# Attention with a position bias and a split-float16 feed-forward layer on one core: six spread maxima, each as one product with the unit matrix instead of a transpose and a spreading product

## The chip, the cores and the metric

The kernel runs on one core of a Trainium2 chip. The metric is device microseconds of one execution. The core has a matrix engine (TensorE, PE in the profile, its weight loads PEld), VectorE (DVE), ScalarE (ACT), GpSimd (POOL) and SyncE (SP), which here only issues transfers. Each engine works through its own instructions in the order in which they stand, and the engines wait for each other by semaphores.

## The reference

```python
def _attn_ref(q, k, v, w1, b1, w2):                      # q, k, v: 4 x 8 x 576 x 64
    scores = scale * np.matmul(q, k.transpose(0, 1, 3, 2))
    ...
    x = (psi_rel / psi_i)[..., None]                     # from the distance of two positions
    bias = np.maximum(x @ w1 + b1, 0.0) @ w2             # one bias table for each of 8 heads
    scores = scores + bias.transpose(2, 0, 1)[None, :, :, :]
    attn = softmax(scores)
    return np.matmul(attn, v)

def _moe_ref(x, w_in, w_out):                            # x: 2304 x 512, d_ff: 2048
    h = x @ w_in
    g = h * np.clip(h + 3.0, 0.0, 6.0) / 6.0
    return g @ w_out
```

The weights `w_in` and `w_out` come as 64-bit floats, which the kernel takes apart itself.

## The kernel before, in words

**Work.** Attention runs in tiles of 128 queries by 576 keys of one head, 144 tiles in 32 units. Of one tile: the scores `s_ps` (line 532 for the first 32 tiles of batches 0 and 1, line 552 for the others), bias and row minimum on DVE (line 564, 0.75 us), the exponential on ACT (line 575), a transpose of the result (`t_ps`, line 623, put away by ACT in line 626; later tiles by a DMA, line 640), and the product with v (`pv_ps`, lines 665 and 711). The attention result of 256 or 320 queries of all four head pairs is the input `x` of one pass of the feed-forward layer: 16 tiles `h_ps` of 12 products (line 786), the clipped product in lines 776, 769, 763 and 765, then four tiles `o_ps` of 48 products (line 809). There are eight such passes.

**Preparation of the weights.** Float16 products need a value and a remainder, so each operand is scaled by a power of two and split into a high part (lines 118 to 124) and a low part (line 141). `w_in` is loaded in 8 chunks and `w_out` in 8 chunks of 1024 KB (line 247). A chunk is treated by ACT (line 257), POOL (258), and DVE (265, 268, 271), gives a row scale (209, 164, 214) and is split into `wi` or `wo`. The loads of `w_out` land in places that the work on earlier chunks has to free first: the first two chunks go into the part of `wo` in which the last two chunks of `w_in` were staged, so each of these two loads waits for the low split (line 141) of one of them; the fourth waits for DVE's line 271 of the first, and so on.

**The spread maximum.** Six times the kernel needs the largest value over all 128 partitions, in every partition: for `v` of the batches 0 to 3 (`v_scale`), for the row scales of `w_in` and for those of `w_out` (`row_ratio`). `spread_max` (lines 145 to 161) takes the maximum of each partition (`m`, line 147), turns the column into a row on TensorE (153), takes the maximum of the row on DVE (155, one value `g`), spreads it over the partitions with a product with a row of ones (157) and copies it out of PSUM (160) into `p`. All this goes through one bank of the pool `w`, which has two banks at that time and also holds `h_ps` and `pv_ps`. With `p` of `w_in` the rows of `x` are scaled (line 1110), with `p` of `w_out` the 16 tiles `g` of the first pass (line 122 on DVE, 124 on ACT), before its first `o_ps`.

**What sets the order.** The kernel is written as generators: `v_scale`, `w_in_prep`, `w_out_prep`, the bias tables and the feed-forward layer are each advanced by a step, up to their next `yield`, from the loop over attention tiles. A scheduler then puts the instructions of each engine into an order by these places and by the times that it assumes for them. From tile 39 on the order of PE stands as written, from tile 45 on that of SP. All loads are issued by SP, in order.

Of the kernel before, what the change touches and what calls it, by code (L numbers as in the profile page):

```python
# [10 lines left out]
F32 = mybir.dt.float32  # L11
# [4 lines left out]
ALU = mybir.AluOpType  # L16
AX = mybir.AxisListType
# [16 lines left out]
def attention_moe_kernel(  # L34
# [16 lines left out]
    nc = tc.nc  # L51
# [7 lines left out]
    const = ctx.enter_context(tc.tile_pool(name="const", bufs=1))  # L59
# [30 lines left out]
    def w_bank(name):  # L90

        if name == "o_ps":
            out_open[:] = [True, 0]
        elif out_open[0] and four[0]:
            while out_open[0] and out_open[1] == 3:
                next(queue[0])
            out_open[1] += 1
        return pools["ps_w"].tile([128, 512], F32, tag="w", name=name)

    open_psum(stack_p, 3, 2)  # L100
    eye_sb = const.tile([128, 128], F32, name="eye_sb")
# [2 lines left out]
    wo = big.tile([128, 2, KF, DM], F16, name="wo")  # L104
    bias_d = [dr_p.tile([H, min(128, S - i), S], F32, name=f"bias{i}") for i in range(0, S, 128)]

    ones_sb = const.tile([1, 128], F32, name="ones_sb")
    b1_sb = const.tile([128, 1], F32, name="b1_sb")
    w2_sb = const.tile([128, 32], F32, name="w2_sb")
    tq = [const.tile([128, 2, 128], F32R, name=f"tq{r}") for r in range(2)]  # L110
# [34 lines left out]
    def spread_max(parts, name, mask=False):  # L145
        m = const.tile([128, 1], F32, tag="m", bufs=2, name=f"m_{name}")
        nc.vector.tensor_reduce(out=m, in_=parts, op=ALU.max, axis=AX.X)
        if mask:
            mb = m.bitcast(U32)
            nc.vector.tensor_single_scalar(out=mb, in_=mb, scalar=0x7F800000, op=ALU.bitwise_and)  # L150
        yield
        ps = w_bank("m_ps")
        nc.tensor.transpose(ps[0:1, 0:128], m, eye_sb)
        g = const.tile([1, 1], F32, tag="gm", bufs=2, name=f"g_{name}")
        nc.vector.tensor_reduce(out=g, in_=ps[0:1, 0:128], op=ALU.max, axis=AX.X)
        yield
        nc.tensor.matmul(out=ps[:, 128:129], lhsT=ones_sb, rhs=g)
        yield
        p = const.tile([128, 1], F32, name=f"p_{name}")
        nc.vector.tensor_copy(out=p, in_=ps[:, 128:129])  # L160
        return p

    def to_pow2(p):
# [4 lines left out]
    def v_scale(b):  # L168
        parts = const.tile([128, PAIRS], F32, tag="vparts", name="vparts")
        for p in range(PAIRS):  # L170
            if b:
                t = st_p.tile([128, VC], F32, tag="vs", bufs=2, name="va")
            elif p < 2:
                t = v_t[0, p, 0] = v_p.tile([128, VC], F32, tag="vh", name="vf")
            else:
                t = v_t[0, p, 0] = st_p.tile([128, 1024], F32, tag="st", name="vf")[:, 0:VC]
            with behind():
                dq("v").dma_start(out=t, in_=vp[b, p])
            yield
            nc.vector.tensor_reduce(  # L180
                out=parts[:, p:p + 1], in_=t, op=ALU.max, axis=AX.X, apply_absolute_value=True
            )
        p = yield from spread_max(parts, f"v{b}", mask=True)
        to_pow2(p)
        s = const.tile([128, 1], F32, name=f"s_v{b}")
        nc.vector.reciprocal(out=s, in_=p)
        pscale[f"v{b}"] = (p, s)
# [28 lines left out]
    def row_ratio(p, name):  # L216
        pm = yield from spread_max(p, name)
        rm = const.tile([128, 1], F32, name=f"rm_{name}")
        nc.vector.reciprocal(out=rm, in_=pm)
        r = const.tile([128, p.shape[1]], F32, name=f"r_{name}c")  # L220
        nc.vector.tensor_scalar(out=r, in0=p, scalar1=rm, scalar2=None, op0=ALU.mult)
        pscale[name] = pm
        pscale["r" + name[1]] = r
# [807 lines left out]
    nc.sync.dma_start(out=eye_sb, in_=eye)  # L1031
    nc.sync.dma_start(out=T[:, 0:512], in_=ltab[:, 0:512])
    nc.vector.memset(cv_sb, 0.0)
    nc.vector.memset(ones_sb, 1.0)
    nc.vector.memset(c36[:, 0:1], 3.0 * CQ)
    nc.vector.memset(c36[:, 1:2], 6.0 * CQ)
    for r in range(2):
# [1 line left out]
    for cs in (slice(512, LT), slice(0, 512)):  # L1039
        nc.vector.tensor_scalar(  # L1040
            out=T[:, cs], in0=T[:, cs], scalar1=w1_sb, scalar2=None, op0=ALU.mult
# [219 lines left out]
```

## Time and profile before

| | |
|---|---|
| three runs | 696.44, 697.87, 702.76 us, median 697.87 |
| the profiled execution | 696.51 us, of it 694.5 us from the first to the last instruction |
| busy in the span: PE, DVE, ACT, POOL | 638.2 (92%), 485.6 (70%), 487.7 (70%), 261.7 us (38%) |
| busy of 16 DMA engines, q1 (SP's queue) | 65.4% of the span |

A busy share is a mean over stages that are limited by different engines. In the slices of the page DVE and ACT are busiest in the first quarter, PE from there to the end.

### The profile page before, as it was taken

To read this page: it belongs to the slowest core of one execution; us is meant where nothing else is said; L and a number is where in the kernel's file an instruction comes from. 1 tells how busy PE (TensorE), PEld (TensorE's weight loads), DVE (VectorE), ACT (ScalarE), POOL (GpSimd) and SP (SyncE) were. 2 spreads that over 40 slices of the span, in tenths; PEclk is the share of its full clock that TensorE was granted. 3 is DMA by queue.
4 is the path that set the end of the run, shared out by engine and by line. 5 is a ranking of instruction groups with operands and counts; after the bars stand their busy time and mean duration, and the time that the engine had idled before them with its cause. 6 is when DMAs were issued, how large, how long until landed. Compare 5 with 4: busy or idle time off the path is not lost. (4 is left out here: it accounts for less than half of the span.)

```text
span 694.5 us, 15117 instructions
## 1 busy us (share of the span) xinstructions
PE 638.2 (92%) x5558; PEld 453.0 (65%) x5558; DVE 485.6 (70%) x1157; ACT 487.7 (70%) x968; POOL 261.7 (38%) x322
## 2 busy tenths in 40 slices
PE   7677899875999989999899999999999999999998
PEld 2223456653687667677788778767776777777775
DVE  7889868899846977667868887777587757710310
ACT  7987778976747987688668867886588757721620
POOL 1112125765413442246335623563365424410420
PEclk9999999998899999999999999999999999999999
DMA  8898779742893989999999899869787895400000
GB/s 294 297 329 325 268 268 337 263 130 77 230 245 93 215 229 210 236 211 206 225 258 266 167 216 191 192 142 210 169 195 136 191 177 122 91 15 29 1 10 28
DMA packets 175737, 130.13 MB, mean 187 GB/s; under 512 B 137520, under 2 KB 144944, under 8 KB 174640
## 3 DMA queue, kind: packets, MB, share of 16 engines
q1 hardware_dynamic: 165872, 113.84, 65.4%
q10 hardware_dynamic: 9792, 15.34, 7.4%
q8 instruction: 43, 0.70, 0.4%
q14 instruction: 30, 0.25, 0.1%
HBM read 77.24 MB, written 15.34 MB: 133 GB/s over the span
## 5 line engine op out<-in xcount | busy, mean ns | idle before, releaser
L786 PE MATMUL h_ps<-x,wi 128*128 128x256 f16 (+1 forms) x1536 | 200.9, 288 | 7.6 <-DVE t L769 4.0
L809 PE MATMUL o_ps<-g,wo 128*128 128x256 f16 (+1 forms) x1536 | 195.7, 286 | 1.6 <-ACT g L763 1.0
L786 PEld LDWEIGHTS <-wi 128*128 128x128 f16 x1536 | 147.7, 98 | 58.1 <-issue 18.7
L809 PEld LDWEIGHTS <-wo 128*128 128x128 f16 x1536 | 147.2, 98 | 47.2 <-issue 10.0
L765 POOL TENSOR_TENSOR g<-t,g 128x256 f16<-128x256 f32 (+1 forms) x128 | 105.5, 834 | 153.8 <-ACT g L763 152.2
L575 ACT ACTIVATE bt<-bt,sm 128x576 f32<-128x576 f32 x144 | 110.4, 767 | 41.2 <-DVE sm L564 39.4
L141 DVE SCALAR_TENSOR_TENSOR hl<-bt,sm,hl 128x576 f16<-128x576 f32 x112 | 99.1, 896 | 20.8 <-POOL hl L118 12.8
L769 DVE SCALAR_TENSOR_TENSOR t<-t,t,h_ps 128x320 f32<-128x320 f32 (+1 forms) x112 | 55.8, 515 | 47.6 <-ACT t L776 46.4
L763 ACT ACTIVATE g<-t 128x256 f16<-128x256 f32 (+1 forms) x128 | 55.4, 439 | 36.3 <-DVE t L769 35.5
L564 DVE CUSTOM_DVE_ANT_0 bt<-s_ps,bt 128x576 f32<-128x576 f32 x88 | 64.5, 750 | 22.0 <-PE s_ps L552 14.7
L118 POOL TENSOR_SCALAR hl<-bt,sm 128x576 f16<-128x576 f32 x56 | 46.7, 835 | 80.1 <-ACT bt L575 18.7
L418 POOL TENSOR_TENSOR qkl<-st,qkh 128x576 fp32r<-128x576 f32 (+2 forms) x48 | 58.5, 1238 | 37.5 <-ACT qkh L411 30.3
L776 ACT ACTIVATE t<-h_ps,t,hr 128x320 f32<-128x320 f32 (+1 forms) x112 | 64.3, 586 | 7.2 <-PE h_ps L786 2.9
L819 ACT ACTIVATE ot<-o_ps,os 128x256 f32<-128x256 f32 (+1 forms) x32 | 15.9, 497 | 64.7 <-PE o_ps L809 57.5
L868 PE MATMUL b_ps<-z_e,w_sb 128*32 128x288 f32 x448 | 45.4, 430 | 15.3 <-POOL x L699 5.9
L583 DVE TENSOR_SCALAR sm<-sm 128x1 f32<-128x1 f32 x112 | 16.9, 151 | 46.5 <-ACT bt L575 46.2
L124 ACT ACTIVATE hl<-bt,sm 128x576 f16<-128x576 f32 x56 | 43.0, 769 | 7.4 <-DVE sm L587 4.5
L851 DVE TENSOR_SCALAR z_e<-T,nbp 128x576 f32<-128x576 f32 x69 | 40.9, 638 | 1.9 <-PE b_ps L868 1.7
L884 ACT ACTIVATE bo<-b_ps,cv_sb,isc 128x288 f32<-128x288 f32 (+1 forms) x52 | 35.0, 674 | 4.3 <-DMA bias<-bo 2.4
L868 PEld LDWEIGHTS b_ps<-z_e,w_sb 128*32 128x32 f32 x448 | 14.9, 111 | 34.2 <-ACT z_e L855 6.8
L258 POOL TENSOR_SCALAR w<-w 128x1024 f32<-128x1024 f32 x8 | 12.2, 1522 | 64.3 <-ACT wo L257 58.2
L855 ACT ACTIVATE z_e<-T,bp 128x576 f32<-128x576 f32 x43 | 32.4, 769 | 5.0 <-DVE bp L1043 2.8
(132 smaller groups left out, 895.9 us busy)
## 6 DMA issues: line engine op xcount, KB each, us to landing
bt<-bias SPq DMA_DIRECT2D x36, 576.0 KB, 5.5
bias<-bo ACTq DMA_DIRECT2D x36, 288.0 KB, 5.7
w<-in_w_in_dram SPq DMA_DIRECT2D x8, 1024.0 KB, 7.1
vs<-in_vp_dram SPq DMA_DIRECT2D x24, 320.0 KB, 5.2
st<-in_qk_dram SPq DMA_DIRECT2D x16, 448.0 KB, 4.0
wo<-in_w_out_dram SPq DMA_DIRECT2D x5, 1024.0 KB, 6.6
bt<-bias SPq DMA_DIRECT2D x16, 288.0 KB, 3.3
qk<-in_qkd_dram SPq DMA_DIRECT2D x8, 544.0 KB, 9.1
```

What stands on the lines that cost most here:

```text
L118: nc.gpsimd.tensor_scalar(out=out, in0=full, scalar1=scale, scalar2=1.0, op0=ALU.mult, op1=ALU.mult)
L141: nc.vector.scalar_tensor_tensor(out=out, in0=full, scalar=scale, in1=high, op0=ALU.mult, op1=ALU.subtract)
L418: nc.gpsimd.tensor_sub(out=lo[:, c:c + w], in0=t[:, c:c + w], in1=hi[:, c:c + w].bitcast(F32))
L564: nc.vector.tensor_tensor_reduce(out=halves(bt), in0=ps, in1=halves(src), op0=ALU.add, op1=ALU.min, scale=-0.125, scalar=3.0e38, accum_out ...
L575: nc.scalar.activation(out=bt, in_=bt, func=AF.Exp, scale=-1.0, bias=sm[:, 0:1], accum_out=total)
L763: nc.scalar.activation(out=g[:, 0], in_=uu, func=AF.Copy)
L765: e.tensor_sub(out=g[:, 1], in0=uu, in1=g[:, 0])
L769: nc.vector.scalar_tensor_tensor(out=t_t[f], in0=t_t[f], scalar=cols(f)[2], in1=h_t.pop(f)[:, 0:n], op0=ALU.min, op1=ALU.mult,)
L776: nc.scalar.activation(out=t_t[f], in_=h_t[f][:, 0:n], func=AF.Relu, scale=cols(f)[0], bias=cols(f)[1],)
L786: nc.tensor.matmul(out=h_t[f][:, 0:n], lhsT=wi[:, a, c, f * 128:(f + 1) * 128], rhs=x[:, e, c], start=(k == 0), stop=(k == 3 * KC - 1),)
L809: nc.tensor.matmul(out=ops[:, 0:n], lhsT=wo[:, a, f, e * 128:(e + 1) * 128], rhs=g_t[f][:, r], start=(f == 0 and a == 0 and r == 0), stop= ...
L868: nc.tensor.matmul(out=pss[a][32 * k:32 * k + 32, 0:HALF], lhsT=w2_sb, rhs=z[:, a * HALF:(a + 1) * HALF],)
```

## The change

Each spread maximum becomes one product and one maximum. The column `m` is read as a 128 x 128 matrix that repeats it in every column (a broadcast access), and stands as the weights; the unit matrix is what moves through. Every row of the result then holds all 128 values of `m`, and a maximum along each row gives `p` in every partition. The one-value tile `g`, the row of ones and the copy are gone, and with them two of the three places at which the generator yields.

```diff
-    ones_sb = const.tile([1, 128], F32, name="ones_sb")
...
         yield
+
         ps = w_bank("m_ps")
-        nc.tensor.transpose(ps[0:1, 0:128], m, eye_sb)
-        g = const.tile([1, 1], F32, tag="gm", bufs=2, name=f"g_{name}")
-        nc.vector.tensor_reduce(out=g, in_=ps[0:1, 0:128], op=ALU.max, axis=AX.X)
-        yield
-        nc.tensor.matmul(out=ps[:, 128:129], lhsT=ones_sb, rhs=g)
-        yield
+        nc.tensor.matmul(out=ps[:, 0:128], lhsT=m.to_broadcast([128, 128]), rhs=eye_sb)
         p = const.tile([128, 1], F32, name=f"p_{name}")
-        nc.vector.tensor_copy(out=p, in_=ps[:, 128:129])
+        nc.vector.tensor_reduce(out=p, in_=ps[:, 0:128], op=ALU.max, axis=AX.X)
         return p
...
-    nc.vector.memset(ones_sb, 1.0)
```

The scheduler makes another order of it between the first spread maximum and the last. Behind the last one, on every engine, the instructions stand as before. In the changed kernel line numbers are lower by 5 behind line 160 and by 6 behind line 1034. Three places:

On SP, the loads between the last chunk of `w_in` and the tiles after it. Before (`wo` is a chunk of `w_out`, `bt` a bias table, `qk` and `vf` operands of attention):

```order
L247 DMA wo<-in_w_out_dram 128x2x1024
L493 DMA bt<-bias_97 128x2x576
L394 DMA qk_874<-in_qkd_dram 128x1088
L447 DMA vf<-in_vp_dram 128x640
L247 DMA wo<-in_w_out_dram 128x2x1024
L493 DMA bt<-bias_98 128x2x576
```

And now:

```order
L242 DMA wo<-in_w_out_dram 128x2x1024 x2
L488 DMA bt<-bias_97 128x2x576
L389 DMA qk_872<-in_qkd_dram 128x1088
L442 DMA vf<-in_vp_dram 128x640
L488 DMA bt<-bias_98 128x2x576
L242 DMA wo<-in_w_out_dram 128x2x1024
```

The second chunk of `w_out` stands right behind the first, ahead of three loads for attention (576, 544 and 320 KB), and the next chunk also stands earlier.

On DVE, behind the scaling of `x` with the maximum of `w_in`. Before (564 is the softmax step of a tile, two rows each; 265 and 268 are the first passes over chunks of `w_out`):

```order
L564 ISA bt,sm<-s_ps,bt 128x576
L564 ISA sm 128x1
L696 TENSOR_TENSOR xr<-pv_ps,xr 128x256
L564 ISA bt,sm<-s_ps,k_531 128x576
L564 ISA sm 128x1
L564 ISA bt,sm<-s_ps,k_531 128x576
L564 ISA sm 128x1
L1110 TENSOR_SCALAR x<-x,r_w1c 128x2x256
L265 TENSOR_SCALAR cu,w2top<-cu 128x1024
```

And now:

```order
L559 ISA bt,sm<-s_ps,bt 128x576
L559 ISA sm 128x1
L260 TENSOR_SCALAR cu,w2top<-cu 128x1024 x2
L263 SCALAR_TENSOR_TENSOR cu<-cu,wo 128x1024
L204 TENSOR_SCALAR w2p<-w2top 128x1
L559 ISA bt,sm<-s_ps,k_529 128x576
L559 ISA sm 128x1
L204 TENSOR_SCALAR w2p<-w2top 128x1
L691 TENSOR_TENSOR xr<-pv_ps,xr 128x256
L559 ISA bt,sm<-s_ps,k_529 128x576
```

Three passes over the first two chunks of `w_out` now stand ahead of two softmax steps and of 696. ACT's line 257 for the same two chunks stands ahead of two of its copies of line 626 in the same way. From here to the maximum of `w_out` the work on `w_out` stands earlier against the softmax steps.

On DVE, at the maximum of `w_out`. Before:

```order
L155 TENSOR_REDUCE g_w_1702<-m_ps 1x1
L141 SCALAR_TENSOR_TENSOR wo<-cu,w2s,wo 128x1024
L851 TENSOR_SCALAR z_e<-T,nbp 128x576 x2
L141 SCALAR_TENSOR_TENSOR hl<-bt,sm,hl 128x576
L160 COPY p_w_1705<-m_ps 128x1
L219 RECIPROCAL rm_w_1707<-p_w_1705 128x1
L202 TENSOR_SCALAR os_1768<-hs_1001,p_w_1705 128x1
L769 SCALAR_TENSOR_TENSOR t<-t,c_121,h_ps 128x256
L202 TENSOR_SCALAR os_2232<-hs_2228,p_w_1705 128x1
L221 TENSOR_SCALAR r_w2c<-w2p,rm_w_1707 128x8
```

And now:

```order
L155 TENSOR_REDUCE p_w_1688<-m_ps 128x1
L140 SCALAR_TENSOR_TENSOR wo<-cu,w2s,wo 128x1024
L846 TENSOR_SCALAR z_e<-T,nbp 128x576 x2
L140 SCALAR_TENSOR_TENSOR hl<-bt,sm,hl 128x576
L214 RECIPROCAL rm_w_1690<-p_w_1688 128x1
L197 TENSOR_SCALAR os_1751<-hs_990,p_w_1688 128x1
L197 TENSOR_SCALAR os_2215<-hs_2211,p_w_1688 128x1
L197 TENSOR_SCALAR os_3454<-hs_3450,p_w_1688 128x1
L559 ISA bt,sm<-s_ps,bt 128x576
L559 ISA sm 128x1
L216 TENSOR_SCALAR r_w2c<-w2p,rm_w_1690 128x8
```

The maximum itself stands where the first maximum stood, but the reciprocal of it is still behind the same four passes, and `r_w2c`, which the scaling of `g` reads, now stands behind a softmax step. On ACT an exponential (line 575) now stands ahead of the scaling of `g`.

## Rows read from the trace of the kernel before

**Rows 1.** Busy time of each engine in four stretches (us from the span's start).
```profile
core 0: us, PE busy (x) PEld busy (x) DVE busy (x) ACT busy (x) POOL busy (x), PEclk, DMA share, GB/s
76.00:132.00 56.00, 53.04 (x390) 32.83 (x390) 42.74 (x117) 44.56 (x87) 22.73 (x21) 0.97 0.78 278
132.00:172.00 40.00, 27.46 (x225) 19.86 (x224) 39.72 (x86) 31.84 (x60) 24.67 (x22) 0.95 0.38 122
172.00:226.00 54.00, 52.88 (x478) 37.53 (x478) 36.35 (x90) 34.51 (x64) 16.59 (x18) 0.94 0.72 187
226.00:694.00 468.00, 451.47 (x4076) 339.78 (x4076) 300.62 (x729) 313.93 (x667) 185.93 (x250) 1.00 0.73 161
```

**Rows 2.** Groups by line and shape, spread maxima: busy us, mean ns | idle before.
```profile
L155 DVE TENSOR_REDUCE g_v<-m_ps 1x1 f32<-1x128 f32 x4 | 1.1, 274 | 0.0
L160 DVE COPY p_v<-m_ps 128x1 f32<-128x1 f32 x4 | 0.6, 150 | 0.8 <-PE m_ps L157 0.8
L157 PE MATMUL m_ps<-g_v,ones_sb 1*128 1x1 f32 x8 | 1.5, 256 | 0.0
L153 PE MATMUL m_ps<-eye_sb,m_v 128*1 128x128 f32 x4 | 1.1, 272 | 0.0
```

**Rows 3.** The same view: a product of a broadcast column with the unit matrix, and a longer maximum.
```profile
L676 PE MATMUL pv_ps<-eye_sb,r_sb 128*64 128x128 f32 x64 | 6.3, 288 | 0.0
L180 DVE TENSOR_REDUCE vparts<-va 128x1 f32<-128x640 f32 x12 | 9.7, 810 | 5.9 <-DMA va<-in_vp_dram 5.9
```

**Rows 4.** What DVE waited for, 76 to 132 us: total us, times, longest.
```profile
DVE bt L564 <- PE s_ps L532: 4.8, 2, 2.8
DVE vparts L180 <- DMA va<-in_vp_dram: 2.4, 2, 1.3
DVE cu L265 <- ACT cu L257: 2.2, 1, 2.2
DVE wi L141 <- ACT wi L124: 1.6, 1, 1.6
DVE p_v L160 <- PE m_ps L157: 0.6, 1, 0.6
```

**Rows 5.** SP's issues of two chunks (start us), and their KB and us to landing.
```profile
86.18 0.37 SPq L247 DMA_DIRECT2D wo<-in_w_out_dram  x1
88.65 0.40 SPq L247 DMA_DIRECT2D wo<-in_w_out_dram  x1
...
wo<-in_w_out_dram SPq DMA_DIRECT2D x1, 1024.0 KB, 5.0
...
wo<-in_w_out_dram SPq DMA_DIRECT2D x1, 1024.0 KB, 9.9
```

**Rows 6.** Timeline, those two chunks on ACT and DVE: start us, us [idle before <-releaser].
```profile
98.65 2.22 ACT L257 ACTIVATE cu<-wo 128x1024 f32<-128x1024 f32 x2 [1.00 <-DMA wo<-in_w_out_dram]
...
99.84 1.22 DVE L265 TENSOR_SCALAR_CACHE_REDUCE cu<-cu 128x1024 f32<-128x1024 f32 x1 [2.19 <-ACT cu L257]
```

**Rows 7.** Timeline of DVE, the fourth scaling of x and a later gap.
```profile
107.26 1.00 DVE L1110 TENSOR_SCALAR x<-x,r_w1c 128x512 f16<-128x512 f16 x1
...
131.08 0.76 DVE L564 CUSTOM_DVE_ANT_0 bt<-s_ps,bt 128x576 f32<-128x576 f32 x1 [2.85 <-PE s_ps L532]
```

**Rows 8.** Timeline of all engines at the maximum of w_out.
```profile
172.76 0.14 DVE L147 TENSOR_REDUCE m_w<-w2p 128x1 f32<-128x8 f32 x1
...
172.87 1.18 PE L868 MATMUL b_ps<-z_e,w_sb 128*32 128x288 f32 x4 [5.86 <-POOL x L699]
...
175.20 0.27 DVE L155 TENSOR_REDUCE g_w<-m_ps 1x1 f32<-1x128 f32 x1
...
176.35 2.38 PE L786 MATMUL h_ps<-x,wi 128*128 128x256 f16 x12
...
179.07 0.16 DVE L160 COPY p_w<-m_ps 128x1 f32<-128x1 f32 x1 [0.82 <-PE m_ps L157]
...
179.97 0.22 DVE L221 TENSOR_SCALAR r_w2c<-w2p,rm_w 128x8 f32<-128x8 f32 x1
...
180.29 4.99 ACT L124 ACTIVATE g<-g,r_w2c 128x512 f16<-128x512 f16 x8
...
183.23 0.50 PE L809 MATMUL o_ps<-g,wo 128*128 128x256 f16 x3
```

## The prediction

> **What bounds the kernel now.** I read the busy times by stretch first [rows 1]. The reader should see who has no idle time left in each stretch. From 132 to 172 us DVE is busy 39.72 of 40 us: it sets the pace. From 172 to 226 PE is busy 52.88 of 54, and from 226 to the end 451.47 of 468. From 76 to 132 nobody is full: PE has 53.04 of 56, ACT 44.56, DVE 42.74, so DVE, which is about to become the bound, leaves 13.3 us unused. So the path to the end runs through DVE's work on the weights up to the column `m_w` of `w_out` at 172.76 [rows 8], and from there through PE. The last spread maximum lies at the end of PE's stretch that closes at 226; behind it the order is the same on every engine, and DMA is busy 0.72 in the stretch ahead of it, so no backlog of transfers waits there. What is won or lost by 226 is therefore carried to the end. Next come DVE's waits from 76 to 132, since that is what can be won [rows 4]: 4.8 us for scores of PE, 2.4 for loads of `v`, 2.2 for the first chunk pass of `w_out` on ACT, 1.6 for the high split of `w_in`, and only 0.6 for the spread maximum itself. Last, the transfers of two chunks [rows 5] and the timeline at the maximum of `w_out` [rows 8].
>
> **The change, part by part: the operations.** Each of the six maxima drops DVE's maximum of one row (274 ns) and its copy (150 ns), PE's transpose (272 ns) and a spreading product in two passes (256 ns each) [rows 2]. It adds one product in two passes and one maximum of 128 values along 128 rows.
>
> - DVE's new maximum is not in the trace. Below it stands the old one, 274 ns, which reads as many values from a row, also from PSUM; above it a maximum over 640 values of all 128 rows, 810 ns [rows 3]. I take 274, as the length of a row is the same; the upper end would add 6 x 0.54 = 3.2 us to DVE. The copies save at most 6 x 0.15 = 0.9 us, less where the next instruction starts before their end; I take 0.5.
> - The new product has the form of line 676, where a broadcast column also stands as weights against the unit matrix: 288 ns a pass [rows 3], there with 64 columns of weights, here with 128. Two passes in a row are at least the transpose's 272 ns, at most 0.58 plus a weight load for each, some 0.9 us. Against 0.27 + 0.51 before, PE gains or loses at most some 0.5 us for each maximum, and for four of the six PE has idle time beside it [rows 1]. I take nothing.
>
> A rule speaks against this part. The Trainium skill (TensorE: Matmul & The Clock Gate, Terms) says that the transpose mode is four times faster for FP32 than a product. By that rule a product of this size would cost 4 x 0.27 = 1.1 us where the transpose cost 0.27, an estimate; with the 0.51 of the spreading product gone, each maximum would cost PE 0.3 us more, and the two that lie in PE's full stretch would add 0.6 us to the sum. The rows show a pass of line 676 at 288 ns and a transpose at 272, and two passes a product, so a factor of about two; nothing here shows four.
>
> **The waits.** In a maximum DVE used to come back to PE and wait: 0.6 us at the `v` of batch 1 [rows 4], 0.8 at `w_out` [rows 8]. The first is inside the next term; the second is weighed with the hand-over below.
>
> **The order: the first chunks of `w_out`.** This is the largest term. With the 0.6 us of wait gone and a softmax step (0.76 us, the duration in [rows 7]) moved behind the last row scale of `w_in`, the last splits of `w_in` come about 1.4 us earlier. Each of them frees the place of one chunk of `w_out`, so the two loads start at about 84.8 and 85.9 instead of 86.18 and 88.65, and the second no longer stands behind three loads for attention. Alone, the first chunk took 5.0 us; the second took 9.9, landing at 98.6 [rows 5], and ACT waited for it 1.00 us until 98.65, DVE then 2.19 until 99.84 [rows 6]. The first landed at 91.2, so between the landings 7.4 us went for that chunk and the 1440 KB ahead of it, 333 KB per us. Behind the first chunk alone the second needs 3.1 us more: it lands at about 93, 5.6 earlier.
>
> So the passes of lines 265 and 268, moved ahead of two softmax steps, find their data when DVE comes to them, and DVE's 2.2 us of waiting for them go. I then walked down DVE's new order, with each row's old duration and PE's and ACT's new orders beside it. The fourth scaling of `x`, old start 107.26 [rows 7], comes out at about 104. Of the waits in [rows 4] go 0.6 + 2.2, some 1.1 of the 1.6, and the 2.4 for loads of `v`, because passes over `w_out` now stand ahead of these maxima: 6.3 us. Two come anew: 2.5 us at about 105, where a softmax step has to wait for scores that PE now computes behind 16 products of `h_ps` and a transpose, and some 0.8 us of short dependences. Net 3.0. Of the 2.85 us at 131.08 [rows 7], which are a wait for scores too, I take half, 1.4, since two more passes over `w_out` now stand ahead. Sum of the gaps: 4.4 us. What the moved rows delay is the softmax: by my walk the steps at 104 to 109 come 1 to 2 us later. That costs nothing as long as DVE is full from 132 to 172 with work that does not wait for them; without that cover it costs these 2 us.
>
> **The hand-over at `w_out`.** Before, `m_w` starts at 172.76, the maximum of the row at 175.20, the copy at 179.07, `r_w2c` at 179.97, the scaling of `g` on ACT at 180.29 [rows 8]. The maximum now gives `p` itself, about 3 us before the old copy. But the reciprocal is still behind four passes (lines 141 and 851, twice each), which before filled most of the time from 175.47 to 179.07, so it gains only the wait and the copy, 0.5 after one small row. Then a softmax step of 0.76 us stands ahead of `r_w2c`, and an exponential of about that length ahead of the scaling on ACT: about 0.5 later in all than before. The first `o_ps` stands at 183.23, 2.9 us behind the first scaling, and PE is busy meanwhile, so the 0.5 is covered; if PE had nothing else, it would cost 0.5. I take 0.
>
> **The sum.** 0.5 for the copies, 4.4 for the gaps, 0 for PE and for the hand-over: 4.9 us. Against the profiled execution, 694.5 us of span and 2.0 around it: 696.5 - 4.9 = 691.6. The median of the runs is 1.4 above the profiled one, so the forecast for a median is 692.9; this likeliest case itself spans a gain of 2 to 7.5, 690.4 to 695.9.
>
> **Rivals.**
>
> - *The gaps only move (chance 0.24).* Against the walk stands that 4.8 of the 13.3 us were waits for scores, and that the softmax, now later, feeds both. If each gap closed opens another, only the copies and the wait at `w_out` remain: gain 0 to 1.5, about 697.
> - *ACT blocks behind the chunk (0.13), the slower one.* ACT's two passes of line 257 now stand ahead of two copies of line 626. If the second chunk lands as before at 98.6 and not at 93, ACT stands until 100.8 with the transposes not put away, PE gets no bank for scores, and DVE idles to 99.84 as before, now with two softmax steps, line 696 and one scaling of `x` (2 x 0.76 + 0.4 + 0.35 = 2.3 us) still to do behind it. Price 2.3 us on DVE, up to 7 if the late softmax leaves DVE idle beyond 132: 700 to 705. It decides from a landing of about 98 on. For it: the transfer that is ahead in the queue took 9.9 us. Against it: what made that long was the three loads that now stand behind.
> - *More of the gaps close (0.16).* All of the 13.3 us but the 3.3 of new waits, with PE's 5.86 us of idle time ahead of 172.87 and its slow stretch behind it (12 products in 2.38 us, mean clock 0.94) in part [rows 1, 8]: gain 7.5 to 11, about 688.5.
>
> The forecast has 0.47. **Range:** 687 to 699 leaves out the upper end of the third rival's gain and most of the second one. A measurement of this kernel can tell about 1%, 7 us, from no change: faster than 690.9 is the last rival and a little of the forecast's own lower end, 0.24; slower than 704.9 is the far end of the second, 0.05, to which I add 0.02 for an order that goes wrong where I did not walk; the same, 0.69.
>
> **What would show it.** Right: the second `w_out` load landing near 93, line 265 on DVE starting near 93 to 95 without the 2.2 us wait; DVE's idle time from 76 to `m_w` some 4 us less than 13.6; `m_w` near 168; the same distance from `m_w` to the first `o_ps`; and from the last spread maximum to the end the same time as before, about 470 us. Wrong: a new wait of ACT or DVE for a transfer at 93 to 100, DVE idle in 132 to 172, PE idle behind the first `o_ps` for `g`, or a product of 128 columns that takes over 1 us.

## The result, and the profile after

The changed kernel takes **701.37 us** (median of 22 runs, 697.86 to 710.67; the longest was a slow execution and is left out of the ratio), the kernel before 697.88 beside it: a ratio of **1.0063, 95% interval 1.0043 to 1.0082**. It is 3.5 us slower, where 5 us less were forecast; the time lies above the range. The profiled execution of after took 699.26 us, 2.75 more than that of before (696.51).

Busy time in the same four stretches, as in [rows 1]:
```profile
core 0: us, PE busy (x) PEld busy (x) DVE busy (x) ACT busy (x) POOL busy (x), PEclk, DMA share, GB/s
76.00:132.00 56.00, 52.17 (x372) 31.90 (x371) 48.41 (x118) 44.58 (x87) 25.37 (x22) 0.95 0.75 271
132.00:172.00 40.00, 31.69 (x253) 22.59 (x253) 37.06 (x86) 32.86 (x61) 25.54 (x20) 0.93 0.36 120
172.00:226.00 54.00, 51.79 (x467) 36.63 (x459) 32.86 (x83) 32.58 (x62) 13.77 (x18) 0.97 0.72 184
226.00:694.00 468.00, 453.81 (x4084) 340.38 (x4078) 302.74 (x731) 314.29 (x667) 186.90 (x250) 1.00 0.73 161
```
From 76 to 132 DVE does 5.7 us more work than before. From 132 to 172 it is no longer full (2.94 us idle), and from 172 to 226 PE is busy for 1.1 us less of the 54.

The groups of the new maximum, in place of those of [rows 2]:
```profile
L153 PE MATMUL m_ps<-eye_sb,m_v 128*128 128x128 f32 x8 | 2.1, 344 | 0.0
L155 DVE TENSOR_REDUCE p_v<-m_ps 128x1 f32<-128x128 f32 x4 | 1.1, 286 | 0.0
L153 PE MATMUL m_ps<-eye_sb,m_w 128*128 128x128 f32 x4 | 1.0, 326 | 0.0
L153 PEld LDWEIGHTS m_ps<-eye_sb,m_w 128*128 128x128 f32 x4 | 0.6, 186 | 0.8 <-issue 0.5 <-ACT atf L621 0.4
```
What DVE waited for from 76 to 132, beside [rows 4] (the four rows left out are 0.3 to 0.5 us each):
```profile
DVE bt L559 <- PE s_ps L527: 5.4, 3, 2.9
DVE x L1104 <- POOL x L694: 0.6, 1, 0.6
...
```
The waits for the chunk, for the split of `w_in`, for loads of `v` and for the spread maximum are gone; those for scores stay. The two chunks (SP, ACT, DVE; [rows 5 to 7] before):
```profile
84.16 2.00 SPq L242 DMA_DIRECT2D wo<-in_w_out_dram  x2
...
92.44 2.21 ACT L252 ACTIVATE cu<-wo 128x1024 f32<-128x1024 f32 x2 [1.48 <-DMA wo<-in_w_out_dram]
...
93.89 1.21 DVE L260 TENSOR_SCALAR_CACHE_REDUCE cu<-cu 128x1024 f32<-128x1024 f32 x1
...
103.58 0.35 DVE L1104 TENSOR_SCALAR x<-x,r_w1c 128x512 f16<-128x512 f16 x1 [0.57 <-POOL x L694]
...
106.63 0.76 DVE L559 CUSTOM_DVE_ANT_0 bt<-s_ps,bt 128x576 f32<-128x576 f32 x1 [2.02 <-PE s_ps L527]
```
The hand-over at `w_out`, all engines, against [rows 8]:
```profile
170.33 0.14 DVE L146 TENSOR_REDUCE m_w<-w2p 128x1 f32<-128x8 f32 x1
...
170.72 0.49 PE L153 MATMUL m_ps<-eye_sb,m_w 128*128 128x128 f32 x2
...
173.52 0.28 DVE L155 TENSOR_REDUCE p_w<-m_ps 128x1 f32<-128x128 f32 x1
...
178.97 4.99 ACT L123 ACTIVATE g<-g,r_w2c 128x512 f16<-128x512 f16 x8
...
183.87 0.55 ACT L771 ACTIVATE t<-h_ps,c,hs 128x256 f32<-128x256 f32 x1
...
187.24 0.41 ACT L758 ACTIVATE g<-t 128x256 f16<-128x256 f32 x1
...
188.72 0.67 POOL L760 TENSOR_TENSOR g<-t,g 128x256 f16<-128x256 f32 x1
...
191.06 0.82 DVE L175 TENSOR_REDUCE vparts<-va 128x1 f32<-128x640 f32 x1 [2.59 <-DMA va<-in_vp_dram]
191.80 0.35 DVE L121 TENSOR_SCALAR g<-g,r_w2c 128x512 f16<-128x512 f16 x1
```
Up to 178.97 this is earlier than before. The rows from 183.87 on are the way of the last of the 16 `g` tiles: its relu `t` on ACT, behind the eight scalings; its two halves on ACT and POOL; its scaling on DVE, behind maxima of the next `v` that wait for loads. Before, the same tile passed ahead of all that:
```profile
178.83 0.56 ACT L776 ACTIVATE t<-h_ps,c,hs 128x256 f32<-128x256 f32 x1 [0.85 <-POOL g L765]
179.96 0.42 ACT L763 ACTIVATE g<-t 128x256 f16<-128x256 f32 x1 [0.57 <-DVE t L769]
...
180.46 0.67 POOL L765 TENSOR_TENSOR g<-t,g 128x256 f16<-128x256 f32 x1 [1.67 <-ACT g L763]
...
185.13 0.35 DVE L122 TENSOR_SCALAR g<-g,r_w2c 128x512 f16<-128x512 f16 x1
```
So the tile is ready 6.7 us later (191.80 against 185.13), though `m_w`, the first scaling on ACT and the first `o_ps` are 1 to 3 us earlier. PE behind its first `o_ps`, after:
```profile
180.09 2.14 PE L804 MATMUL o_ps<-g,wo 128*128 128x256 f16 x18
182.16 0.67 PE L863 MATMUL b_ps<-z_e,w_sb 128*32 128x288 f32 x2
182.76 0.83 PE L804 MATMUL o_ps<-g,wo 128*128 128x256 f16 x6
183.52 0.67 PE L863 MATMUL b_ps<-z_e,w_sb 128*32 128x288 f32 x2
184.12 2.47 PE L804 MATMUL o_ps<-g,wo 128*128 128x256 f16 x21
...
192.20 0.49 PE L804 MATMUL o_ps<-g,wo 128*128 128x256 f16 x3 [1.47 <-DVE g L121]
193.43 2.04 PE L863 MATMUL b_ps<-z_e,w_sb 128*32 128x288 f32 x16 [0.74 <-DVE z_e L846]
```
and before, where 45 and then 60 products of `o_ps` run without a wait:
```profile
186.71 5.09 PE L809 MATMUL o_ps<-g,wo 128*128 128x256 f16 x45
...
192.08 1.18 PE L868 MATMUL b_ps<-z_e,w_sb 128*32 128x288 f32 x16
193.19 6.72 PE L809 MATMUL o_ps<-g,wo 128*128 128x256 f16 x60
```
Small groups cost more for each product (2 products of `b_ps` take 0.67 us, 16 of them 1.18), and two waits, 1.47 and 0.74 us, come on top. A measure for the kernels here is the time from `m_w` to the 191st `o_ps` (some 210 us into the span), up to which PE has the same work in both: 37.2 us before (172.76 to 209.92), 40.6 after (170.33 to 210.91). This is used below as **the distance**.

So the difference of the profiled executions is made of -2.43 at `m_w`, +3.42 over the distance, +0.55 to the fifth output eviction (261.23 before, 262.77 after) and +1.30 from there to the eighth (292.30 and 295.14), in all 2.84; the spans differ by 3.0. The 1.30 come about at a wait of PE near 291, before and after:
```profile
291.18 1.17 PE L868 MATMUL b_ps<-z_e,w_sb 128*32 128x288 f32 x12 [1.60 <-ACT z_e L855]
```
```profile
294.01 2.00 PE L863 MATMUL b_ps<-z_e,w_sb 128*32 128x288 f32 x12 [2.31 <-ACT z_e L850]
```
ACT is late there because two copies of `tq` that stand ahead of `z_e` in its order wait for a load, in both kernels:
```profile
288.66 0.52 ACT L431 ACTIVATE tq<-st 64x64 fp32r<-64x64 f32 x2 [2.50 <-DMA st<-in_qk_dram]
```
```profile
291.50 0.52 ACT L426 ACTIVATE tq<-st 64x64 fp32r<-64x64 f32 x2 [2.48 <-DMA st<-in_qk_dram]
```

### The profile page after: what moved, and what is told of

Read it like the earlier page. It is cut to its first block, busy times and chain, and to the rows that moved or that the text cites. A ratio compares the mean times of both kernels' runs of the same rounds, so it can differ in the third digit from the quotient of the medians.

```text
span 697.5 us, 15099 instructions
## 1 busy us (share of the span) xinstructions
PE 646.9 (93%) x5552; PEld 457.4 (66%) x5552; DVE 488.1 (70%) x1150; ACT 487.5 (70%) x968; POOL 261.9 (38%) x322
## 5 line engine op out<-in xcount | busy, mean ns | idle before, releaser
L760 POOL TENSOR_TENSOR g<-t,g 128x256 f16<-128x256 f32 (+1 forms) x128 | 107.3, 848 | 154.3 <-ACT g L758 152.7
L758 ACT ACTIVATE g<-t 128x256 f16<-128x256 f32 (+1 forms) x128 | 55.4, 439 | 37.2 <-DVE t L764 36.5
L863 PE MATMUL b_ps<-z_e,w_sb 128*32 128x288 f32 x448 | 50.1, 451 | 11.9 <-ACT z_e L850 4.1
L863 PEld LDWEIGHTS b_ps<-z_e,w_sb 128*32 128x32 f32 x448 | 16.8, 115 | 32.9 <-ACT z_e L850 8.3
L253 POOL TENSOR_SCALAR w<-w 128x1024 f32<-128x1024 f32 x8 | 10.7, 1337 | 65.4 <-ACT wo L252 52.8
```

Of the source, the lines that this page charges most:

```text
L758: nc.scalar.activation(out=g[:, 0], in_=uu, func=AF.Copy)
L760: e.tensor_sub(out=g[:, 1], in0=uu, in1=g[:, 0])
L863: nc.tensor.matmul(out=pss[a][32 * k:32 * k + 32, 0:HALF], lhsT=w2_sb, rhs=z[:, a * HALF:(a + 1) * HALF],)
```

## Experiments

Each kernel was timed in 12 executions beside the kernel before. Ratios are to before, whose median beside them was 697.3 to 698.1. A ratio is good to some 0.2 or 0.3%, that is 1.5 to 2 us. Each trace is one execution.

**The old and the new maximum mixed.** The kernels of this part are `before` with, ahead of the old code of the maximum,
```
+        if name in ("w2",):
+            nc.tensor.matmul(out=ps[:, 0:128], lhsT=m.to_broadcast([128, 128]), rhs=eye_sb)
+            p = const.tile([128, 1], F32, name=f"p_{name}")
+            nc.vector.tensor_reduce(out=p, in_=ps[:, 0:128], op=ALU.max, axis=AX.X)
+            return p
```
for other names: `("w2",)` is the maximum of `w_out` alone (only_w2), `("v1",)` that of batch 1's `v` at 76 us (only_v1), `("v0", "w1")` the first two (v0_w1). With `if name != "w2":` (not_w2), `"v1"` (not_v1) or `"v3"` (not_v3, the last maximum) it is after but for that one.

> The kernel before with the new product and row maximum for the w_out maximum alone; the five others stay a transpose and a spreading product. Hand-over theory: this alone turns the order behind the w_out maximum, so that on DVE a maximum over a v load (vparts) that waits for its transfer stands ahead of the last scaled tile of g, and PE waits 1 to 2.5 us for that tile near 195; the time goes up by 2 to 3.5 us, to 700 to 701.5, and the rows of PE up to the first o_ps are those of before. Theory that the early reorder (second v maximum) costs it: 698, within 0.7 us of before. Theory that the operations themselves cost about 0.6 us each: 698.5, with no new wait of PE behind the first o_ps.

> The kernel after with the old transpose and spreading product for the w_out maximum alone. Hand-over theory: the early gain stays (m_w of w_out 2 to 2.5 us earlier than before) and the wait behind the first o_ps is gone, so 695 to 696, 2 to 3 us under before. Early-reorder theory: the loss stays, 700.5 to 701.5. Operations theory: five of six prices, 700.5 to 701, and m_w of w_out no earlier in the sum.

> The kernel before with the new product for the second v maximum alone (m_v at 76 us), which is the one that moves both first w_out loads ahead on SP. Hand-over theory: early gain without the loss, 695 to 696. Early-reorder theory: nearly the whole loss, 700.5 to 701.5. Operations theory: one of six prices, 698.5.

> The kernel after with the old transpose and spreading product for the second v maximum alone; SP and POOL keep the order of before. Hand-over theory: no early gain, the loss behind the w_out maximum stays, 700 to 702. Early-reorder theory: 697.5 to 698, as before. Operations theory: five of six prices, 700.5 to 701, without a new wait of PE behind the first o_ps.

Measured: only_w2 698.42 us (1.0019, 0.9991 to 1.0047), not_w2 700.22 (1.0031, 0.9999 to 1.0062), only_v1 700.97 (1.0048, 1.0020 to 1.0075), not_v1 700.34 (1.0040, 1.0013 to 1.0068). None of the three theories on record fits all four. only_w2 costs 1.1 us, and its interval reaches below 1; the three others cost 2.9 to 3.7 each, most of the whole, so the parts do not add. The distance is 37.6 in only_w2, 36.7 in not_w2 and 37.4 in not_v1: the long one of after is there only where the maxima of batch 1's `v` and of `w_out` are both new. In only_v1 it reads 42.0, but that says nothing: `m_w` stands earlier in PE's work there (12 products of `h_ps` and 16 of `pv_ps` more lie behind it), and the 191st `o_ps` comes 1.3 us earlier than before (208.59). So not_w2, not_v1 and only_v1 lose their time behind 210 us, and the traces say where PE waits: 2.03 us near 212 for an output eviction in not_w2, 1.35 near 239 for ACT in not_v1, and near 291 4.4 us in not_w2, 2.2 in not_v1 and 3.75 in only_v1.

The cost of the operations by themselves: v0_w1 changes two maxima, and the order stays but for a handful of rows.

> The kernel before with the new product and row maximum for the first v maximum and the w_in maximum alone. These two leave the order of PE, ACT, POOL and SP of before as it is but for a handful of rows, so this prices the operations without the reorder. Order theory: within 0.7 us of before, 697 to 698.4. Operations theory: two of six prices of about 0.6 us, 698.8 to 699.5.

Measured: 697.20 us (0.9993, 0.9975 to 1.0012). Its groups, old and new in one kernel:
```profile
L158 PE MATMUL m_ps<-eye_sb,m_v 128*1 128x128 f32 x3 | 0.8, 271 | 0.0
L154 PE MATMUL m_ps<-eye_sb,m_v 128*128 128x128 f32 x2 | 0.4, 275 | 0.0
L154 PEld LDWEIGHTS m_ps<-eye_sb,m_v 128*128 128x128 f32 x2 | 0.3, 191 | 0.0
L156 DVE TENSOR_REDUCE p_v<-m_ps 128x1 f32<-128x128 f32 x1 | 0.3, 286 | 0.0
```
A pass of the product takes 275 ns beside the transpose's 271, and the maximum 286 ns. The rows leave the operations no price that would make after slower, and the time shows none within its interval (1.3 us). The second version of this test, v0_w1_tq below, agrees less well.

**Two suspected waits.** In before_out2 and after_out2 the output tile has two buffers:
```
-            ot = f_p.tile([128, gw], F32, tag="o", bufs=1, name="ot")[:, 0:n]
+            ot = f_p.tile([128, gw], F32, tag="o", bufs=2, name="ot")[:, 0:n]
```
since the fourth eviction of the output, 210.82 before and 211.44 after, waits in both kernels for the store of the third, which could swallow a lead.

In before_tq and after_tq the two copies of `tq` for the first unit of attention are GpSimd's:
```
-            nc.scalar.activation(out=tz[rows, 0, rows], in_=t[rows, c], func=AF.Copy)
+            if b == 0 and p == 0:
+                nc.gpsimd.tensor_copy(out=tz[rows, 0, rows], in_=t[rows, c])
+            else:
+                nc.scalar.activation(out=tz[rows, 0, rows], in_=t[rows, c], func=AF.Copy)
```

> The kernel before with two output tiles ot in place of one; the order of every engine is that of before. Output-tile theory: the early gain of every variant is given back because ACT's fourth output eviction waits for the landing of the third store, up to 210.7 in before and 209.6 to 211.8 in the variants; with two tiles that wait of 5.25 us at 210.82 goes, and the time falls by 0.5 to 2 us, to 695.5 to 697. Transfer-at-291 theory: within 0.7 us of before. Operations or clock theory: within 0.7 us of before.

> The kernel after with two output tiles ot in place of one; the order of every engine is that of after. Output-tile theory: both waits of ACT for the output store (6.14 us at 207.46 and 3.51 us at 211.44) go, PE reaches the products of 212 to 250 earlier by 1 to 2.5 us, and the time falls by 2 to 4 us, to 697.5 to 699.5. Transfer-at-291 theory: less than 1 us. Operations or clock theory: still 3 to 4 us over the kernel before.

> The kernel before with the two small copies of the first tq on POOL in place of ACT, so that ACT does not wait there for the load of st; the order of all else is that of before. Transfer-at-291 theory: ACT's wait of 2.50 us at 288.66 and PE's of 1.60 us at 291.18 go; the time falls by 1 to 2 us. Output-tile theory: no more than 1.6 us, the wait itself. Operations or clock theory: no more than 1.6 us as well, and the distance to the changed kernel stays at 3 to 4 us.

> The kernel after with the same two copies on POOL; the order of all else is that of after. Transfer-at-291 theory: PE's wait of 2.31 us at 294.01 goes and with it the stretch of 294 to 298 at half the clock (12 products in 2.00 us); the time falls by 2.5 to 4 us, to 697.5 to 699, and the distance to the kernel before with the same edit is 1 to 2 us. Output-tile theory: falls by 2 to 3 us and keeps about 1.5 us of distance from the stretch up to 250. Operations or clock theory: the distance to the kernel before with the same edit stays at 3 to 4 us.

Measured: before_out2 696.57 (0.9990, 0.9966 to 1.0013) and after_out2 702.64 (1.0069, 1.0043 to 1.0095): in these two orders the output tile is not it. before_tq **693.41** (0.9939, 0.9916 to 0.9962) and after_tq 697.01 (1.0012, 0.9981 to 1.0042): the wait near 291 costs about 4 us in *both* orders (4.4 in each by the medians, 4.3 and 3.6 by the ratios), so it is a loss that both kernels have, and 3.6 us stay between them. GpSimd now stands where ACT stood:
```profile
287.98 0.53 POOL L432 CAST tq<-st 64x64 fp32r<-64x64 f32 x2 [1.85 <-DMA st<-in_qk_dram]
```
and PE's ten us from 290 are busy 9.48 instead of 8.43. The profile of before had shown this wait as 1.6 us, and the time it is worth is nearly three times that; the last section comes back to it.

These traces also show what a lead is worth. The four profiled executions in before's order (before, and with either or both of these edits) have `m_w` at 172.8, 171.0, 171.3 and 173.0 and distances of 37.2, 36.7, 37.3 and 37.4. A lead at `m_w` is there again, more or less, at the fifth output eviction: before_tq is 1.5 us ahead of before at `m_w` and 1.3 there, before_out2 1.8 and 2.3. In after's order (after, after_tq, after_out2) `m_w` lies at 170.3, 169.7 and 167.7, and the distance is 40.6, 40.6 and 40.5: some 3.4 us more, whenever `m_w` comes.

**The late tile.** after_g makes the maxima of the last batch's `v` wait for the last `g` tile, so that DVE scales it first:
```
+            if b == 3 and g_last:
+                nc.vector.tensor_copy(out=parts[:, p:p + 1], in_=g_last.pop()[:, 0, 0:1])
...
+            g_last.append(g_t[KF - 1])
```
after_g_tq adds the copies of `tq`, and the two kernels of `_out2` the second output buffer. not_v3_g is not_v3 with this edit: in after, PE waits 0.90 us for DVE at 228 behind the last maximum, which not_v3 gives its old place.
```profile
228.12 2.78 PE L781 MATMUL h_ps<-x,wi 128*128 128x256 f16 x24 [0.90 <-DVE t L764]
```

> The kernel after with one copy of a single column that makes the four maxima over the last batch of v wait, on DVE, for the last scaled tile of g; PE and POOL keep the order of after, on DVE that tile and three z_e now stand ahead of the maxima. Theory that the lead is lost behind the first o_ps: PE's waits of 1.47 us at 192.20 and 0.74 us at 193.43 go, the second output eviction comes 2.5 to 3.5 us earlier than in after (200.85), and the time falls by 2 to 3.5 us, to 698 to 699.5. Theory that the cause lies later (transfers at 211 and 291) or in the clock: the early gain shows at 200 but the time falls by less than 1 us.

> The same with the two copies of the first tq on POOL. Theory that the lead is lost behind the first o_ps: the two edits add up, 4.4 us for tq (as measured) and 2 to 3.5 us for the tile of g, so 693.5 to 695, within 1.5 us of the kernel before with the tq edit (693.41). Theory that the cause lies later or in the clock: 696 to 697.5, no better than the tq edit alone (697.01).

> The kernel before with the tq copies on POOL and two output tiles. If the two add up: 692 to 693 (4.35 and 1.2 us under before). If the wait for the output store only holds what waits for something else anyway: 693.4, as with the tq edit alone.

> The kernel after with all three edits. With the stall behind the first o_ps gone, the lead of 2.4 us at m_w can pass the output evictions: 690.5 to 693, at or under the kernel before with the same two edits that apply to it. If the lead is lost elsewhere again: 694 to 697.

> The kernel after with the old transpose and spreading product for the last v maximum (at 220 us) alone; the order differs from after only between 218 and 230. Order theory: the wait of PE for t (0.9 us at 228.12, in every variant with this maximum new and in none with it old) goes, the products of 235 to 248 start 0.5 to 1.5 us earlier than in after against the second output eviction, and the time falls by 0.5 to 1.5 us, to 700 to 701. Operations theory: one price less, 700.8. Theory that all is the phase of transfers behind 250: no change beyond the noise.

> The same with the last scaled tile of g ahead of the v maxima on DVE. From the first o_ps to the second output eviction 19.1 us as in the earlier run of that edit (21.0 in after, 15.4 in before), and no 0.9 us wait for t near 228. Order theory: both repairs reach the end, 697.5 to 699.5. Theory that transfers behind 200 set the pace: the distance at 248 us is that of after all the same (1.5 us behind before) and the time stays at 700 to 701.

> The same with the two copies of the first tq on POOL, the edit that took 4.4 us from before and from after alike. Order theory: 693 to 694, as the kernel before with that edit (693.41). Operations theory: 694.5 to 695.

| kernel | median us | ratio (95%) | distance us |
|---|---|---|---|
| after_g | 701.08 | 1.0047 (1.0016 to 1.0078) | 38.7 |
| after_g_tq | 699.41 | 1.0022 (0.9995 to 1.0050) | 38.7 |
| after_g_tq_out2 | 695.34 | 0.9971 (0.9942 to 0.9999) | 38.7 |
| before_tq_out2 | **693.34** | 0.9940 (0.9919 to 0.9960) | 37.4 |
| not_v3 | 700.52 | 1.0051 (1.0026 to 1.0076) | 40.9 |
| not_v3_g | 699.62 | 1.0029 (1.0007 to 1.0051) | 38.7 |
| v0_w1_tq | 695.35 | 0.9967 (0.9948 to 0.9985) | 37.5 |

The edit takes 1.9 of the 3.4 us out of the distance each time, and the wait of `o_ps` for `g` with it. It stops there since the tile itself is late (DVE, after_g):
```profile
188.88 0.84 DVE L121 TENSOR_SCALAR g<-g,r_w2c 128x512 f16<-128x512 f16 x1 [1.69 <-POOL g L764]
```
In the time little of it arrives: 0.3 us alone, 0.85 for the last maximum alone, 1.75 for both, which the noise all but covers, and 2 us over before stay. That was the outcome on record for a cause that lies later or in the clock. The traces show one place where the gain goes. From the 191st `o_ps` to the fifth output eviction takes 51.3 us in before and 51.9 in after, but 53.5 in after_g, 53.3 in after_tq and 54.7 in after_g_tq and after_g_tq_out2. PE waits there near 240 for ACT, 0.6, 1.5, 2.0 and 3.0 us in these four, and ACT for a transfer (after_g_tq_out2):
```profile
237.39 0.77 ACT L123 ACTIVATE hl<-bt,sm 128x576 f16<-128x576 f32 x1 [2.84 <-DMA at<-hl]
...
240.39 1.47 PE L788 MATMUL h_ps<-x,wi 128*128 128x256 f16 x12 [3.01 <-ACT bo L887]
```
In not_v3_g (53.0) it is 0.89 us near 214 for an output eviction instead. The misses belong here too: after_g_tq came out 2.4 us *above* after_tq, though its distance is shorter (its profiled execution is late already at `m_w`, 174.4). v0_w1_tq came out 1.9 us above before_tq, which is what the theory of a price of the operations had forecast. Its trace does not show such a price: against before_tq it loses 2.3 us between the fifth and the eighth output eviction (31.2 us instead of 28.9), far behind both maxima. But by the times alone the two pairs do not exclude 1 us.

after_t mends the first step of the tile's way: the scalings read a copy of the row ratios that depends on the 16th tile's high part, so that its relu stands ahead of them. after_t_tq has the copies of `tq` moved too.
```
+            r2 = const.tile([128, KF // 2], F32, name="r2_late")
+            nc.vector.tensor_copy(out=r2[:, 0:1], in_=g_t[KF - 1][:, 0, 0:1])
+            nc.vector.tensor_copy(out=r2, in_=pscale["r2"])
             for f in range(KF):
-                high_part(g_t[f], g_t[f], pscale["r2"][:, f // 2:f // 2 + 1], pick("gr", f))
+                high_part(g_t[f], g_t[f], r2[:, f // 2:f // 2 + 1], pick("gr", f))
```

> After, with the scalings of `g` made to depend on the high part of the 16th `g` tile (two small DVE copies), so that ACT's `t` of that tile no longer stands behind the eight scalings of 0.62 us. Theory (the late 16th tile is what eats the lead): from `m_w` to the 191st `o_ps` 37 to 38.5 us as in before's order (37.2) instead of 40.6 in after, no wait of `o_ps` for `g`, and a median 1.5 to 3 us under after's 701.4: 698.5 to 700. Rival (the lead is lost further behind anyway): 37 to 38.5 there too, but the median stays at 700 to 702. Third (the scalings come too late and PE stands ahead of the first `o_ps`): 39 to 41 and no gain.

> The same, and the two `tq` copies of the first unit on GpSimd. Theory: what is left over before_tq (693.4) is the late 16th tile: 694 to 695.5, against 697.0 with the copies moved alone. Rival (lost further behind): 696.5 to 698.

Measured: 702.87 us (1.0065, 1.0038 to 1.0091) and 701.56 (1.0051, 1.0023 to 1.0080), with a distance of 40.8 in both: the third outcome. PE ahead of and behind its first `o_ps`, after_t:
```profile
182.19 2.44 PE L866 MATMUL b_ps<-z_e,w_sb 128*32 128x288 f32 x16 [1.42 <-DVE z_e L849]
186.27 0.68 PE L866 MATMUL b_ps<-z_e,w_sb 128*32 128x288 f32 x4 [1.65 <-DVE z_e L849]
187.21 1.59 PE L866 MATMUL b_ps<-z_e,w_sb 128*32 128x288 f32 x12 [0.26 <-DVE z_e L849]
188.73 0.83 PE L807 MATMUL o_ps<-g,wo 128*128 128x256 f16 x6
```
No `o_ps` waits for `g` any more, but the first stands at 188.7 instead of 180.1, and PE has 3.3 us of waits ahead of it. The wait was moved, not removed, so these two runs do not tell whether the late tile alone makes the distance; they show that not every order with the tile early is a good one.

## Why the prediction was wrong, point by point

**What held.** The place of the early gain: the two loads at 84.2, the second chunk at hand at 92.4 (forecast 93), the pass on DVE at 93.89 without its 2.2 us wait (93 to 95), the fourth scaling of `x` at 103.6 (104), the new wait of 2.0 us at 106.6 (2.5 at 105). The rival in which ACT blocks behind the chunk did not come. The operations: 286 ns for the maximum (274 taken) and 0.39 to 0.49 us for a product (0.27 to 0.9; the one at 128.5 us, at half the granted clock, took 0.79). In the time they show nothing in v0_w1, while v0_w1_tq leaves room for about 1 us.

The Trainium skill (TensorE: Matmul & The Clock Gate, Terms) calls the transpose mode four times faster for FP32, and does not say than what; read as the prediction read it, the product would take 1.1 us, an estimate. Here one whole product takes 0.49 us with its two weight loads, and a pass 275 ns beside 271. The measurement decides: no factor of four in this form.

**A term mis-sized: the gain by `m_w`.** Forecast 4.9 us; the profiled pair shows 2.4 (172.76 to 170.33), and over four profiled executions in before's order (mean 172.0) and eight in after's (170.46) it is 1.5. Single executions scatter by more than that (171.0 to 173.0, and 167.7 to 174.4), so the size is rough. (In the sum itself, 691.6 and 1.4 make 693.0 and not 692.9, which changes nothing.) The gaps of 76 to 132 did close (13.3 to 7.6 us), but 2.9 us opened from 132 to 172, in waits for scores (1.5) and for a chunk's pass on ACT (1.2); "DVE is full from 132 to 172" had been the cover of the later softmax, and after the change it is not. That is the rival in which the gaps only move, by half.

**The step that failed: "what is won or lost by 226 is carried to the end", with the hand-over at 0.** A lead was carried, nearly whole, where the order was the *same* (before_tq). Between `m_w` and 226 the change makes another order, and that is 3.4 us longer. The prediction followed the hand-over to the *first* `o_ps`, which came 3.1 us earlier, even a little better than forecast (from `m_w` 9.8 us instead of 10.5), and called PE busy behind it. It did not follow the *last* of the 16 tiles, on which the 46th to 48th product stand, through ACT, POOL and DVE in the new order, where it is 6.7 us late. "PE idle behind the first `o_ps` for `g`" was named as a sign of the forecast being wrong, and it is what the trace shows, 1.47 us of it. The reason given for "carried to the end" failed too: a mean DMA share of 0.72 was read as "no backlog of transfers", but single transfers stand in the path behind 210 (a store of the output near 212, `at` near 240, `st` near 291), and PE waits behind them.

How sure is each part: that the order from `m_w` to 210 us costs 3.4 us is shown (40.5 to 40.9 in four profiled executions of after's order, not_v3 among them; 36.7 to 37.5 in six of before's, the two of v0_w1 among them); that 1.9 of these are the last scaling's place on DVE is shown by after_g. That the rest is the tile's earlier steps and the smaller groups of `b_ps` is argued from the rows alone. And it is not shown that the distance makes the time: with the gain at `m_w` of 1.5 to 2.4 us against it, after is only 1 to 2 us late at 210 us, the rest of the 3.5 comes about behind, and 1.9 us less of distance (after_g) gave 0.3 us of time.

**"From the last spread maximum to the end the same."** Not quite: the rows behind 230 stand in the same order on every engine, and still after loses 1.3 us more at the wait near 291, where what a kernel loses differs from one to the next (1.4 to 4.4 us of waiting among the 13 kernels here that keep the copies on ACT), as it does near 240. This is probably also why one part undone does not give one part back: the parts of the change do not add.

**What stays open.** How the 3.5 us divide, and about 2 us of not_v3_g's 699.62 over before; its one trace has 1.6 of them between the 191st `o_ps` and the fifth output eviction. Over the executions compared here, before has a median span of 695.7 us with a mean granted clock of 0.9846 (162 of them), after 699.6 with 0.9782 (21). Among the executions of either kernel, 0.001 less of mean clock goes with 0.26 (before) and 0.29 us (after) more of span; at that rate the 0.0064 between the two would be 1.6 to 1.9 of the 3.9 us, an estimate. So part of it is time at the lower clock, but the means do not say behind which wait.

The best version measured is before with the `tq` copies moved (693.41, and 693.34 with the second output buffer), faster than the two kernels by 4.4 and 8 us. It has nothing to do with the change, and the new maximum does not improve it (v0_w1_tq 695.35, after_g_tq_out2 695.34, after_tq 697.01).

## What to carry to other kernels

When an edit moves rows in an in-order schedule, follow the last tile that the next full engine needs, not the first, through every queue of the new order; a lead counts only behind the last row that has moved, and then it still has to pass the waits for transfers that stand behind. Price an edit by a version that changes the operations and keeps the order (here two maxima of six: the rows as short as before, no difference in one pair of timings, 1.9 us in another), and a reorder by the time between two fixed pieces of work on the engine that sets the pace, with the same work between them. And look for the wait that both versions have: it was worth more than the whole change.

## What was not expected of the chip

**A short wait of PE can cost more than its length, and the same wait does not always.** PE's granted clock in the ten us from 290, before and after (columns as in [rows 1]):
```profile
290.00:300.00 10.00, 8.43 (x94) 5.75 (x95) 7.03 (x17) 8.73 (x19) 1.99 (x3) 1.00 0.78 161
```
```profile
290.00:300.00 10.00, 7.69 (x58) 4.28 (x58) 6.40 (x17) 7.28 (x16) 0.66 (x1) 0.83 1.03 171
```
After a wait of 1.60 us PE went on at the full level (2.4 GHz; 12 products of `b_ps` in 1.17 us); after 2.31 us part of the stretch was granted the half level (1.2 GHz), and the 12 products took 2.00 us. In the 13 kernels that keep these copies on ACT, the granted clock of this stretch (in after_t, which comes later, of the ten us around its wait) is 1.00 in five profiled executions, with waits of 1.4, 1.6, 1.7, 2.0 and 2.3 us, and 0.69 to 0.83 in the eight others, with waits of 2.2 to 4.4. So the 1.6 us in the profile of before was a cheap case: without the copies on ACT the median fell by 4.4 us.

A wait farther on shows it with the length held fixed. All 20 kernels have it, 2.31 to 2.34 us, with the same work of PE behind it; before and after_out2:
```profile
343.33 0.53 PE L552 MATMUL s_ps<-qkh 64*128 64x288 f32 x3 [2.33 <-DVE sm L564]
```
```profile
343.71 0.84 PE L547 MATMUL s_ps<-qkh 64*128 64x288 f32 x3 [2.32 <-DVE sm L559]
```
In the ten us from its end the granted clock is 1.00 in eight of the profiled executions (before and after among them), 0.83 or 0.84 in ten (before_tq among them) and 0.68 in two (after_out2 and after_g_tq). From the ninth to the thirteenth output eviction, which holds this wait, they take 67.0, 68.4 to 68.9 and 69.95 us. So 1.5 to 3 us of a profiled execution can be this alone, and two profiled spans do not size a term of 2 us.

**A pass of an FP32 product against the unit matrix is as quick as a transpose**: 275 ns and 271 ns. A product has two passes, and the second overlaps the first, as its weight load does (186 to 191 ns): 0.39 to 0.49 us for both.
